# Attention and channel mix on one core: copies that two engines may do, and a merged sum on VectorE

## The chip, the cores and the metric

The kernel runs on one core of a Trainium2 chip. The metric is the device time of one execution in microseconds (us). The engines are TensorE (PE in the rows; its weight loads are PEld), VectorE (DVE), ScalarE (ACT), GpSimd (POOL) and SyncE (SP, which issues the DMAs).

## The reference

Eight batches of eight heads, 576 positions, 64 columns a head; then a channel mix with 512 model columns and 1024 hidden ones.

```python
scores = (q @ k.T) / sqrt(D)
cum = cumsum(maximum(s, 0))
bias = -(cum[:, :, :, None] - cum[:, :, None, :])
scores = where(causal, -1e6, scores + minimum(bias, 0))
attn = exp(scores - max); attn = attn / (sum(attn) + 1e-9)
x = (attn @ v), heads side by side            # 8 x 576 x 512
x_prev = x shifted by one position
xk = mu_k * x + (1 - mu_k) * x_prev           # xr the same with mu_r
v = maximum(xk @ w_k, 0) ** 2 @ w_v
out = sigmoid(xr @ w_r) * v
```

## The kernel before, in words

The program is first written as a list of tasks and then ordered. `Plan.add` (L113) records for each instruction its engine, its planned time in ns, what emits it, and which earlier tasks it depends on. `Plan.forward` (L135) goes through planned time: whichever engine is free first takes, of its tasks that are ready, the one due first. `Plan.backward` (L248) works out new due times from that order. `Plan.run` (L295) does this 30 times, keeps the order that ends earliest in planned time, and emits it. So each engine has a fixed queue in the order of the plan, and an instruction whose input is late holds up all behind it on its engine. A task has one engine: `act`, `dve`, `pool`, `pe` and `dma` (L363 to L385) record a task for ScalarE, VectorE, GpSimd, TensorE and SyncE with its planned duration. Until the first split scores are due, the plan fills idle time of TensorE with small matmuls on an identity (`one_idle`, L397).

Attention goes by visits, two heads each: the first batch in two halves (8 visits), the second batch (4 visits), the other six (24 visits). In the first 12 visits weights of the softmax are turned on TensorE and copied to SBUF by ScalarE (`turn_plain`, L1304: L1341, L1364). In the last 24 visits, most of the span, `split_scores` (L1086) is used. For each head it has four chains. Three are the query tiles 1 to 3 (`tile_`, L1159): the product of queries and keys into a bank of PSUM named s or t (two of each), the row minimum with the mask on VectorE (`least`, L1105), the exponent and its row sum on ScalarE (`exponents`, L1120), the reciprocal of the sum (`inverses`, L1129: a shifted copy on ScalarE, then a reciprocal on VectorE), and the weights as two f16 halves (`halves`, L1142): the first on ScalarE (L1147), the rest of it on VectorE (L1153), which reads the bank last and so frees it. The fourth chain (`last_and_first`, L1169) has the last tile and the 64 first queries packed into the same 128 rows, so on rows 64 to 127 two sums, of columns LAST and c, belong to one query. They are added across by two ScalarE instructions (L1202) with `upper_rows`, a column of zeros and ones, as scale; on rows 0 to 63 they stay apart. Then a DMA turns the halves (`turn_by_dma`, L1218) and TensorE sums the values (`sum_values`, L1242), whose result ScalarE scales into xT (L1297).

Before its turn, a visit is prepared by `split_qk` (L914) and `split_v` (L858): keys and queries are rounded into KH, KL and G by copies (L936 and L957 on ScalarE for the first two batches, L941 and L962 on GpSimd for the others; L951 on GpSimd), and GpSimd subtracts for the rests (L945, L966). Values are split on GpSimd (L867, L873, L875). The weights of the mix are unpacked ahead in `join` and `parts_of` (L701 on ScalarE, L708 on GpSimd).

The channel mix (`channel_mix`, L1522) goes in 18 chunks of 256 positions, and the plan fills them in between the attention's work as soon as a chunk's heads are done. Per chunk: the mix of x with its predecessor in a bank xp (L1568 on ScalarE, L1575 on VectorE), the f16 halves xh and xl (L1597 on ScalarE, L1601 on VectorE), the hidden product in a bank m (L1631), its relu r (L1643, ScalarE), square (L1653, VectorE), and halves kh (L1659, ScalarE) and kl (L1661, VectorE), the gate (L1675, L1687) and the output product (L1702, L1713). `MARGIN` (L1770) is part of a chunk's first due time.

Of the kernel before, what the change touches and what calls it, by code (L numbers as in the profile page):

```python
# [54 lines left out]
class Plan:  # L55
# [24 lines left out]
    def __init__(self):  # L80
        self.tasks, self.slots, self.due = [], {}, 0.0
        self.columns, self.idle, self.busy_from = {}, None, None
        self.quarters = {}
        self.issues = {}

# [48 lines left out]

    def forward(self, due):  # L135
# [15 lines left out]
        ready = {e: [] for e in engines}  # L151
        for i, t in enumerate(self.tasks):
            if not missing[i]:
                heapq.heappush(coming[t[0]], (0.0, i))
# [16 lines left out]
        while len(order) < n:  # L171
            best = None
            for e in engines:
                if ready[e]:
# [19 lines left out]
            while coming[e] and coming[e][0][0] <= s:  # L194
                _, i = heapq.heappop(coming[e])
                heapq.heappush(ready[e], (due[i], i))
            _, i = heapq.heappop(ready[e])
            if e == "PE" and ready[e]:
# [11 lines left out]
            _, ns, _, _, _, land = self.tasks[i]  # L210
            if e == "PE":
# [27 lines left out]
            for u in users[i]:  # L239
# [4 lines left out]
                if not missing[u]:  # L244
                    heapq.heappush(coming[self.tasks[u][0]], (ready_at[u], u))
        return order, start, max(done), emits

    def backward(self, start):  # L248
# [11 lines left out]
        for i in range(n):  # L260
            if not left[i]:
                heapq.heappush(coming[self.tasks[i][0]], (0.0, i))
        for _ in range(n):
# [15 lines left out]
            _, ns, _, deps, _, _ = self.tasks[i]  # L279
            free[e] = at[i] = s + (max(ns, self.issues.get(i, self.ISSUE)) if e == "SP" else ns)  # L280
            for d in deps:
                k, _, _, _, _, land = self.tasks[d]
# [10 lines left out]
    PASSES = 30  # L293

    def run(self):  # L295
        best = None
        due = [t[4] for t in self.tasks]
        for _ in range(self.PASSES):
# [3 lines left out]
            due = self.backward(found[1])  # L302
        order, _, _, emits = best
        for n, i in enumerate(order):
            for emit in emits.get(n, ()):
                emit()
            self.tasks[i][2]()
# [3 lines left out]
def forgetting_attention_then_channel_mix(  # L311
# [71 lines left out]

    def dma(emit, reads, writes, ns):
# [50 lines left out]
    upper_rows = fixed(const.tile([P, 1], F32, name="upper_rows"))  # L435
    for i in range(2):
        pool(
            lambda i=i: nc.gpsimd.memset(upper_rows.ap[64 * i : 64 * i + 64], 1.0 * i),
            [], [(upper_rows, i)], 1, 100,
        )  # L440
# [258 lines left out]
    def parts_of(block, whole):  # L699
        hi, lo = (block, 0), (block, 1)  # L700
        act(lambda: nc.scalar.copy(block.get()[:, 0], whole.get()), [whole], [hi], 512, 94)  # L701

        def first():
# [7 lines left out]
            [whole, hi], [lo], 512, 190, 2.21,  # L711
# [146 lines left out]
    def split_v(vn, V, scales):  # L858
# [3 lines left out]
        def whole():  # L862
# [10 lines left out]
        pool(lambda: nc.gpsimd.tensor_copy(part(0), whole()), [vn], [(V, 0)], n, 150)  # L873
        pool(
            lambda: nc.gpsimd.tensor_tensor(out=part(1), in0=whole(), in1=part(0), op=ALU.subtract),  # L875
            [vn, (V, 0)], [(V, 1)], n, 210, 2.21,
# [37 lines left out]
    def split_qk(b, hp, qs, k):  # L914
# [6 lines left out]
        for j in range(2):  # L921
# [11 lines left out]
            )  # L933
            if b < BY_DMA:
                act(
                    lambda own=own, K=K: nc.scalar.copy(K.get()[own], k.get()[own]),  # L936
                    [(k, j)], [(K, j)], nk, 90, quarters=(2 * j, 2 * j),
                )
            else:
                pool(  # L940
                    lambda own=own, K=K: nc.gpsimd.tensor_copy(K.get()[own], k.get()[own]),  # L941
                    [(k, j)], [(K, j)], nk, 150, 0.8333, (2 * j, 2 * j),
                )
# [4 lines left out]
                [(k, j), (K, j)], [(K, 1 - j)], nk, 210, 2.21, (2 * j, 2 - 2 * j),  # L948
            )
            pool(  # L950
                lambda own=own, KB=KB: nc.gpsimd.tensor_copy(KB.get()[0:64, 0:nk], k.get()[own]),  # L951
                [(k, j)], [(KB, 0)], nk, 150, 0.8333, (2 * j, 0),
            )
            x = qs[j]
            if b < BY_DMA:
                act(
                    lambda x=x, QQ=QQ: nc.scalar.copy(QQ.get(), x.get()),  # L957
                    [(x, 0), (x, 1)], [(QQ, 0), (QQ, 1)], nq, 90,
                )
            else:  # L960
                pool(
                    lambda x=x, QQ=QQ: nc.gpsimd.tensor_copy(QQ.get(), x.get()),  # L962
                    [(x, 0), (x, 1)], [(QQ, 0), (QQ, 1)], nq, 150,
                )
# [5 lines left out]
                [(x, 0), (QQ, 0)], [(QL, 0)], nq, 210, 2.21,  # L970
# [115 lines left out]
    def split_scores(passes, F, am, top):  # L1086
# [42 lines left out]
        def inverses(i, e, o):  # L1129
            act(  # L1130
                lambda: nc.scalar.activation(
                    rinv.get()[:, i:e], sums.get()[:, o : o + e - i], AF.Copy,
                    bias=1.0e-9 / HALF, scale=1.0 / HALF,
                ),
                [(sums, o + y - i) for y in range(i, e)], [(rinv, y) for y in range(i, e)], 1, 92,
            )
            dve(
                lambda: nc.vector.reciprocal(rinv.get()[:, i:e], rinv.get()[:, i:e]),  # L1138
                [], [(rinv, y) for y in range(i, e)], 1,
            )  # L1140

        def halves(ps, n, i, t, a, step):  # L1142
            def part(y):
                return F.get()[:, a + y * step : a + y * step + n]

            act(
                lambda: nc.scalar.activation(  # L1147
                    part(0), ps.get()[:, :n], AF.Copy, scale=rinv.get()[:, i : i + 1]
                ),
                [ps, (rinv, i)], [(F, (t, 0))], n, 144,  # L1150
# [9 lines left out]
        def tile_(t):  # L1160
# [5 lines left out]
            inverses(t, t + 1, t)  # L1166
            halves(ps, n, t, t, P * OB[t], P * (t + 1))

        def last_and_first():  # L1169
# [30 lines left out]
            for x, y in ((LAST, c), (c, LAST)):  # L1200
                act(
                    lambda x=x, y=y: nc.scalar.activation(  # L1202
                        sums.get()[:, x + 2 : x + 3], sums.get()[:, y : y + 1], AF.Identity,
                        scale=upper_rows.ap, bias=sums.get()[:, x : x + 1],
                    ),
                    [(sums, LAST), (sums, c), (upper_rows, 0), (upper_rows, 1)], [(sums, x + 2)], 1, 92,
# [759 lines left out]
```

## Time and profile before

| | us |
|---|---|
| median of 3 runs | 805.56 (805.26 to 806.03) |
| the profiled execution | 807.22 |
| its span, first to last instruction | 805.5 |
| mean granted TensorE clock in it | 0.991 |

| engine | busy us | share of the span | instructions |
|---|---|---|---|
| TensorE matmul | 768.5 | 95% | 5376 |
| TensorE weight load | 571.6 | 71% | 5376 |
| VectorE | 644.9 | 80% | 2031 |
| ScalarE | 638.0 | 79% | 1939 |
| GpSimd | 420.2 | 52% | 516 |

The time of an execution is a little longer than the span. The weight loader and the matmuls are two rows of one engine, and matmuls overlap in its pipe, so a busy TensorE can still have room. A mean over the span mixes stages: the weights' unpacking and the first heads up to about 160 us, attention with the mix in between up to about 700 us, and the rest of the mix alone.

### The profile page before, as it was taken

Reading aid. Unit: us, or ns where it says so; the run is one execution under the profiler, and the core shown is the slowest. Engines: PE = TensorE matmul, PEld = TensorE weight load, DVE = VectorE, ACT = ScalarE, POOL = GpSimd, SP = SyncE. Lnnn points to the kernel's source line nnn. Section 1 sums busy time; section 2 is a strip of 40 time slices with the busy share of each in tenths; the row PEclk is TensorE's granted clock in tenths of the full one; section 3 lists DMA queues with packets and bytes.
Section 4 is the critical chain, followed back from the end, with each engine's and each line's share of the span. In section 5 each row is a group of like instructions: output and inputs, shape, how many; then the busy total and the mean of one; then the engine's idle time right before and its main releaser. Section 6 shows DMA issues by size and latency. Waiting matters only on the chain. (4 is left out here: it accounts for less than half of the span.)

```text
span 805.5 us, 17398 instructions
## 1 busy us (share of the span) xinstructions
PE 768.5 (95%) x5376; PEld 571.6 (71%) x5376; DVE 644.9 (80%) x2031; ACT 638.0 (79%) x1939; POOL 420.2 (52%) x516
## 2 busy tenths in 40 slices
PE   9989899899989999999999999999999999999998
PEld 7766477676657676767676867676867686777785
DVE  7989976868988898888898988878987988646541
ACT  6799899778988798878888897979888988646521
POOL 6779685466576664564666655665555661000000
PEclk9999799999999999999999999999999999999999
DMA  7784444356896977996888979696879675511100
GB/s 252 214 263 135 157 126 132 114 124 148 180 194 169 183 178 181 202 172 163 164 184 159 218 162 200 164 216 156 208 157 198 158 138 84 133 48 40 40 27 26
DMA packets 220157, 124.16 MB, mean 154 GB/s; under 512 B 180192, under 2 KB 193504, under 8 KB 220064
## 3 DMA queue, kind: packets, MB, share of 16 engines
q1 hardware_dynamic: 220064, 123.06, 66.1%
q8 instruction: 42, 0.69, 0.4%
q14 instruction: 51, 0.42, 0.2%
HBM read 61.21 MB, written 19.33 MB: 100 GB/s over the span
## 5 line engine op out<-in xcount | busy, mean ns | idle before, releaser
L1631 PEld LDWEIGHTS <-w_k 128*128 128x128 f16 x1728 | 162.1, 98 | 35.1 <-issue 14.4
L1702 PE MATMUL m<-w_v,kh 128*128 128x512 f32 x528 | 179.2, 404 | 0.2 <-ACT g L1687 0.2
L1631 PE MATMUL m<-xh,w_k 128*128 128x256 f16 x976 | 175.5, 273 | 3.3 <-DVE kl L1661 2.7
L1631 PE MATMUL m<-xl,w_k 128*128 128x256 f16 x488 | 133.1, 273 | 0.1
L1702 PEld LDWEIGHTS m<-w_v,kh 128*128 128x128 f32 x528 | 98.3, 189 | 20.4 <-ACT g L1687 0.9
L1702 PE MATMUL m<-w_v,kl 128*128 128x512 f32 x264 | 106.7, 404 | 0.0
L945 POOL TENSOR_TENSOR KH<-raw,KH 64x576 fp32r<-64x576 f32 x64 | 90.4, 1413 | 10.1 <-ACT KH L936 5.7
L1568 ACT ACTIVATE xp<-x,shares 128x256 f32<-128x256 f32 (+3 forms) x184 | 78.4, 426 | 21.0 <-DVE xl L1601 11.4
L966 POOL TENSOR_TENSOR QL<-raw,G 64x576 fp32r<-64x576 f32 (+1 forms) x64 | 84.7, 1324 | 15.1 <-PE t L1095 7.7
L1575 DVE SCALAR_TENSOR_TENSOR xp<-x,shares,xp 128x256 f32<-128x256 f32 (+3 forms) x184 | 76.5, 416 | 17.8 <-ACT xp L1568 14.8
L1675 PE MATMUL m<-w_r,xh 128*128 128x512 f16 x264 | 84.5, 380 | 3.5 <-DVE kl L1661 3.0
L1153 DVE SCALAR_TENSOR_TENSOR W<-s,rinv,W 128x64 f16<-128x64 f32 (+2 forms) x144 | 64.9, 456 | 9.9 <-ACT W L1147 8.0
L1122 ACT ACTIVATE s<-s,nm 128x64 f32<-128x64 f32 (+2 forms) x144 | 61.8, 429 | 11.9 <-DVE nm L1107 10.3
L962 POOL CAST G<-raw 128x576 fp32r<-128x576 f32 x48 | 31.9, 665 | 73.6 <-issue 47.0
L1147 ACT ACTIVATE W<-s,rinv 128x64 f16<-128x64 f32 (+2 forms) x144 | 65.2, 460 | 6.3 <-DVE rinv L1138 5.3
L1153 DVE SCALAR_TENSOR_TENSOR W<-t,rinv,W 128x512 f16<-128x512 f32 (+1 forms) x96 | 61.6, 646 | 6.1 <-ACT W L1147 5.9
L1095 PE MATMUL s<-KH,G 128*128 128x64 f32 (+2 forms) x192 | 57.2, 312 | 8.3 <-DVE W L1153 6.4
L1122 ACT ACTIVATE t<-t,nm 128x512 f32<-128x512 f32 (+1 forms) x96 | 55.5, 578 | 6.3 <-DVE nm L1186 2.1
L1601 DVE TENSOR_TENSOR xl<-xp,xh 128x512 f16<-128x512 f32 x72 | 49.3, 685 | 12.6 <-ACT xh L1597 12.5
L1147 ACT ACTIVATE W<-t,rinv 128x512 f16<-128x512 f32 (+1 forms) x96 | 58.2, 614 | 0.9 <-DVE rinv L1138 0.7
L1107 DVE CUSTOM_DVE_ANT_0 t<-t,lower 128x512 f32<-128x512 f32 (+1 forms) x96 | 56.6, 596 | 2.8 <-PE t L1095 1.5
L1597 ACT CAST xh<-xp 128x512 f16<-128x512 f32 x72 | 42.4, 589 | 20.4 <-DVE xp L1575 20.3
(210 smaller groups left out, 1967.0 us busy)
## 6 DMA issues: line engine op xcount, KB each, us to landing
raw<-in_q SPq DMA_DIRECT2D x112, 144.0 KB
raw<-in_k SPq DMA_DIRECT2D x32, 288.0 KB
vn<-in_v SPq DMA_DIRECT2D x24, 384.0 KB
out<-g SPq DMA_DIRECT2D x36, 256.0 KB
x_d<-xT SPq DMA_DIRECT2D x28, 288.5 KB
x<-x_d SPq DMA_DIRECT2D x11, 514.0 KB
w_k<-in_moe_w_k SPq DMA_DIRECT2D x8, 512.0 KB
w_v<-in_moe_w_v SPq DMA_DIRECT2D x8, 512.0 KB
```

The lines of the kernel that those rows point to most:

```text
L945: lambda own=own, other=other, K=K: nc.gpsimd.tensor_tensor(out=K.get()[other], in0=k.get()[own], in1=f32(K.get()[own]), op=ALU.subtract),
L966: lambda x=x, QQ=QQ, QL=QL: nc.gpsimd.tensor_tensor(out=QL.get()[0:64, 0:nq], in0=x.get()[0:64], in1=f32(QQ.get()[0:64]), op=ALU.subtract,),
L1095: lambda x=x, G=G, K=K, r=r: nc.tensor.matmul(ps.get()[:m, :n], G.get()[:r, q : q + m], K.get()[:r, k0 : k0 + n], start=x == 0, stop=x == 1,),
L1107: lambda: nc.vector.tensor_tensor_reduce(out=ps.get()[:, :n], in0=ps.get()[:, :n], in1=mask(), scale=-SCALE, scalar=3.0e38, op0=ALU.add, o ...
L1122: lambda: nc.scalar.activation(ps.get()[:, :n], ps.get()[:, :n], AF.Exp, bias=nm.get()[:, i + o : i + o + 1], scale=-1.0, accum_out=sums.g ...
L1147: lambda: nc.scalar.activation(part(0), ps.get()[:, :n], AF.Copy, scale=rinv.get()[:, i : i + 1]),
L1153: lambda: nc.vector.scalar_tensor_tensor(out=part(1), in0=ps.get()[:, :n], scalar=rinv.get()[:, i : i + 1], in1=part(0), op0=ALU.mult, op1 ...
L1568: lambda z=z: nc.scalar.activation(to(*z), source(1, *z), AF.Copy, scale=share(0, c + z[0])),
L1575: lambda z=z: nc.vector.scalar_tensor_tensor(out=to(*z), in0=source(0, *z), scalar=share(1, c + z[0]), in1=to(*z), op0=ALU.mult, op1=ALU.a ...
L1631: lambda u=u, f=f, c=c, n=n, w=w, x=x: nc.tensor.matmul(ps.get()[:, u * CT : (u + 1) * CT], weight["k", c, f // 4].get()[:, w, f % 4 * P : ...
L1675: lambda c=c, n=n, x=x, w=w: nc.tensor.matmul(ps.get(), x.get()[:, c, ts], weight["r", c, 0].get()[:, w], start=c == 0 and n == 0, stop=c ...
L1702: lambda f=f, n=n, x=x, w=w: nc.tensor.matmul(ps.get(), x.get()[:, f, ts], weight["v", f, 0].get()[:, w], start=f == 0 and n == 0, stop=f ...
```

## The change

A task may get a second engine (`or_on`), with its own planned time and instruction. In `forward` such a task is offered to both engines, and the second takes it only if the first is not free within `LATER`, 300 ns. `backward` takes the engine chosen. The tasks that get a second engine: ScalarE's first halves, xT, turned blocks and corners, the first term of the mix, xh, relu and kh (or VectorE); the weights' first part and the early key and query copies (ScalarE, or GpSimd); the later key and query copies, KL and the values' first part (GpSimd, or ScalarE).

In `last_and_first`, one VectorE reduction adds the two sums on rows 64 to 127 into both columns of a second pair; ScalarE makes the shifted copy for rows 0 to 63 from the first pair and for the others from the second; one reciprocal follows for both columns. `upper_rows` goes. Some planned durations are altered, and `MARGIN` is 5000 instead of 10000.

```diff
+    def or_on(self, i, engine, ns, emit):
+        self.others[i] = engine, ns, emit
...
+        def offer(at, i):
+            heapq.heappush(coming[self.tasks[i][0]], (at, i))
+            if i in self.others:
+                heapq.heappush(coming[self.others[i][0]], (at, i))
...
             _, i = heapq.heappop(ready[e])
+            own = self.tasks[i][0]
+            if e != own and free[own] < s + self.LATER:
+                heapq.heappush(coming[e], (max(s, free[own]) + self.LATER, i))
+                continue
...
+            on[i] = e
+            if e != own:
+                ns = self.others[i][1]
...
     PASSES = 30
+    LATER = 300.0
...
+    def or_act(i, emit, n, extra=51):
+        plan.or_on(i, "ACT", n * 0.8333 + extra, emit)
+
+    def or_dve(i, emit, n, extra=70):
+        plan.or_on(i, "DVE", n / 0.96 + extra, emit)
+
+    def or_pool(i, emit, n, extra=150):
+        plan.or_on(i, "POOL", n * 0.8333 + extra, emit)
...
-        pool(lambda: nc.gpsimd.tensor_copy(part(0), whole()), [vn], [(V, 0)], n, 150)
+        or_act(
+            pool(lambda: nc.gpsimd.tensor_copy(part(0), whole()), [vn], [(V, 0)], n, 150),
+            lambda: nc.scalar.copy(part(0), whole()), n, 70,
+        )
...
-            act(
-                lambda: nc.scalar.activation(
-                    part(0), ps.get()[:, :n], AF.Copy, scale=rinv.get()[:, i : i + 1]
-                ),
-                [ps, (rinv, i)], [(F, (t, 0))], n, 144,
-            )
+            or_dve(
+                act(
+                    lambda: nc.scalar.activation(
+                        part(0), ps.get()[:, :n], AF.Copy, scale=rinv.get()[:, i : i + 1]
+                    ),
+                    [ps, (rinv, i)], [(F, (t, 0))], n, 144,
+                ),
+                lambda: nc.vector.tensor_scalar(
+                    out=part(0), in0=ps.get()[:, :n], scalar1=rinv.get()[:, i : i + 1],
+                    scalar2=None, op0=ALU.mult,
+                ),
+                n, 130,
+            )
...
-            for x, y in ((LAST, c), (c, LAST)):
+            dve(
+                lambda: nc.vector.tensor_reduce(
+                    out=upper(sums, LAST + 2, c + 3),
+                    in_=upper(sums, LAST, c + 1).unsqueeze(1).broadcast_to([64, 2, 2]),
+                    axis=mybir.AxisListType.X, op=ALU.add,
+                ),
+                [(sums, LAST), (sums, c)], [(sums, "u")], 4, quarters=(2, 2),
+            )
+            for rows, o, keys in (
+                (slice(0, 64), LAST, [LAST, c]), (slice(64, P), LAST + 2, ["u"]),
+            ):
                 act(
-                    lambda x=x, y=y: nc.scalar.activation(
-                        sums.get()[:, x + 2 : x + 3], sums.get()[:, y : y + 1], AF.Identity,
-                        scale=upper_rows.ap, bias=sums.get()[:, x : x + 1],
+                    lambda rows=rows, o=o: nc.scalar.activation(
+                        rinv.get()[rows, LAST : c + 1], sums.get()[rows, o : o + 2], AF.Copy,
+                        bias=1.0e-9 / HALF, scale=1.0 / HALF,
                     ),
...
-            inverses(LAST, c + 1, LAST + 2)
+            dve(
+                lambda: nc.vector.reciprocal(rinv.get()[:, LAST : c + 1], rinv.get()[:, LAST : c + 1]),
+                [(rinv, (LAST, "s")), (rinv, (LAST + 2, "s"))], [(rinv, LAST), (rinv, c)], 1,
+            )
...
-    MARGIN = 10000.0
+    MARGIN = 5000.0
```

The other pairs are of the same form. Lines of the changed kernel that the rows below name: L1165 exponents, L1174 and L1262 shifted copies (L1262 the merged chain's), L1191 and L1196 the first half on ScalarE and on VectorE, L1203 the second half, L1181 and L1269 reciprocals, L1251 the reduction, L1361 xT; of the preparation L973 and L1000 copies to KH and G on GpSimd, L988 to KL, L982 and L1009 the subtractions.

What stands in ScalarE's queue around the merged chain of one head, in the middle of attention; before:

```order
L1122 ACTIVATE t_232,sums_147<-t_232,nm_173 128x512
L1122 ACTIVATE s_145,sums_147<-s_145,nm_173 128x64
L1147 ACTIVATE W_2308<-s_152,rinv_2363 128x448
L1202 ACTIVATE sums_147<-sums_147,upper_rows 128x1 x2
L1643 ACTIVATE r_101<-m_272 128x512
L1131 ACTIVATE rinv_2167<-sums_147 128x2
```

and of the change, in such a head:

```order
L1165 ACTIVATE t_229,sums_174<-t_229,nm_233 128x512
L1165 ACTIVATE s_136,sums_174<-s_136,nm_233 128x64
L1262 ACTIVATE rinv_2361<-sums_174 64x2 x2
L1361 ACTIVATE xT_297<-s_142,scales_2419 128x64
L1361 ACTIVATE xT_297<-po_89,scales_2419 128x512
L1191 ACTIVATE W_2326<-s_136,rinv_2361 128x64
```

The pair that adds is gone; two copies on 64 rows each stand right behind the exponents, the second of which reads what VectorE adds. In 30 of the 48 heads the two stand side by side as here, in 18 something is between them.

VectorE's queue in attention, before:

```order
L1661 TENSOR_TENSOR kl_969<-m_272,kh_957 128x512
L1138 RECIPROCAL rinv_2167<-rinv_2167 128x1
L1107 ISA s_145,nm_173<-s_145,lower 128x448
L1107 ISA nm_173 128x1
L1653 SCALAR_TENSOR_TENSOR m_215<-m_215,scaled_1388,r_101 128x512
L1138 RECIPROCAL rinv_2167<-rinv_2167 128x1
L1153 SCALAR_TENSOR_TENSOR W_2136<-t_213,rinv_2167,W_2136 128x320
```

and of the change, where a first half is among the moved:

```order
L1269 RECIPROCAL rinv_2156<-rinv_2156 128x2
L1181 RECIPROCAL rinv_2156<-rinv_2156 128x1
L1659 SCALAR_TENSOR_TENSOR xp_332<-x_180,shares_780,xp_332 128x64
L1809 SCALAR_TENSOR_TENSOR g_430<-g_430,m_201 128x512
L1203 SCALAR_TENSOR_TENSOR W_2119<-s_142,rinv_2156,W_2119 128x64
L1196 TENSOR_SCALAR W_2119<-t_209,rinv_2156 128x320
L1688 TENSOR_TENSOR xl_837<-xp_332,xh_828 128x512
L1203 SCALAR_TENSOR_TENSOR W_2119<-t_229,rinv_2156,W_2119 128x512
L1203 SCALAR_TENSOR_TENSOR W_2119<-t_209,rinv_2156,W_2119 128x320
```

Here VectorE makes both halves of the 320 columns (L1196, then L1203); in all 24 of 240 first halves are VectorE's.

GpSimd's queue while a visit is prepared, before:

```order
L962 CAST G_577<-raw_514 128x576
L941 CAST KH_608<-raw_536 64x576
L966 TENSOR_TENSOR QL_226<-raw_514,G_577 64x576
L945 TENSOR_TENSOR KH_608<-raw_536,KH_608 64x576
L951 CAST KL_626<-raw_536 64x576
L962 CAST G_582<-raw_133 128x576
L941 CAST KH_622<-raw_514 64x576
```

and of the change:

```order
L982 TENSOR_TENSOR KH_769<-raw_480,KH_769 64x576
L988 CAST KL_633<-raw_480 64x576
L910 TENSOR_TENSOR V_2163<-vn_1016,V_2163 128x768
L1000 CAST G_640<-raw_498 128x576
L988 CAST KL_578<-raw_525 64x576
L1009 TENSOR_TENSOR QL_227<-raw_498,G_640 64x576
L982 TENSOR_TENSOR KH_600<-raw_525,KH_600 64x576
```

The copy to KH_600 no longer stands ahead of its subtraction: it is in ScalarE's queue.

## Rows read from the trace of the kernel before

**Rows 1.** The page: busy us (share of the span) and instructions of each engine.
```profile
PE 768.5 (95%) x5376; PEld 571.6 (71%) x5376; DVE 644.9 (80%) x2031; ACT 638.0 (79%) x1939; POOL 420.2 (52%) x516
```

**Rows 2.** Stretches: us, busy us (instructions) of each engine, PEclk, DMA share, GB/s.
```profile
20.00:40.00 20.00, 18.90 (x170) 15.53 (x170) 19.60 (x58) 14.97 (x53) 15.77 (x19) 1.00 0.70 214
...
40.00:80.00 40.00, 36.36 (x288) 27.14 (x284) 36.43 (x122) 37.38 (x103) 33.29 (x39) 0.96 0.64 198
80.00:120.00 40.00, 35.91 (x226) 24.91 (x227) 34.65 (x109) 37.72 (x107) 30.95 (x34) 0.87 0.46 147
...
160.00:680.00 520.00, 499.43 (x3482) 366.93 (x3482) 448.60 (x1470) 444.16 (x1408) 305.77 (x356) 1.00 0.81 173
...
560.00:600.00 40.00, 38.53 (x276) 29.06 (x275) 36.69 (x126) 35.98 (x116) 24.27 (x28) 1.00 0.85 189
...
720.00:805.50 85.50, 81.72 (x510) 62.77 (x508) 38.67 (x65) 33.18 (x63) 0.00 (x0) 1.00 0.10 35
```

**Rows 3.** The chain that ended last: start us, us, what (pieces of it).
```profile
521.43 0.69 ACT sums L1202 x2
...
702.66 2.13 PE po L1270 x28
...
704.86 5.29 PE m L1675 x24
...
801.84 0.69 DVE g L1713
```

**Rows 4.** Waits of PE and PEld, 160 to 704 us: us, times, longest us.
```profile
PE s L1095 <- DVE W L1153: 6.4, 17, 0.8
...
PE t L1095 <- DVE W L1153: 2.9, 6, 0.9
...
PEld s L1095 <- DVE W L1153: 18.3, 38, 1.1
...
PEld t L1095 <- DVE W L1153: 4.8, 11, 1.0
```

**Rows 5.** Waits of DVE, 160 to 704 us.
```profile
DVE rinv L1138 <- ACT rinv L1131: 22.6, 34, 2.4
DVE W L1153 <- ACT W L1147: 13.9, 35, 1.1
```

**Rows 6.** Groups by form, merged chain: out<-in xcount, busy us, mean ns, idle before.
```profile
L1202 ACT ACTIVATE sums<-sums,upper_rows 128x1 f32<-128x1 f32 x96 | 32.1, 388 | 0.1
...
L1131 ACT ACTIVATE rinv<-sums 128x2 f32<-128x2 f32 x48 | 10.0, 208 | 0.2
...
L1186 DVE TENSOR_REDUCE nm<-nm 64x2 f32<-64x4 f32 x48 | 7.4, 154 | 1.5
```

**Rows 7.** Groups by form: pairs of like work on ScalarE and VectorE.
```profile
L1601 DVE TENSOR_TENSOR xl<-xp,xh 128x512 f16<-128x512 f32 x72 | 49.3, 685 | 12.6 <-ACT xh L1597 12.5
...
L1568 ACT ACTIVATE xp<-x,shares 128x256 f32<-128x256 f32 x88 | 42.7, 485 | 13.3 <-DVE xl L1601 6.8 <-DMA x<-x_d 5.6
L1575 DVE SCALAR_TENSOR_TENSOR xp<-x,shares,xp 128x256 f32<-128x256 f32 x88 | 42.6, 484 | 12.4 <-ACT xp L1568 11.2
L1597 ACT CAST xh<-xp 128x512 f16<-128x512 f32 x72 | 42.4, 589 | 20.4 <-DVE xp L1575 20.3
...
L1153 DVE SCALAR_TENSOR_TENSOR W<-t,rinv,W 128x512 f16<-128x512 f32 x48 | 35.8, 746 | 2.3 <-ACT W L1147 2.2
...
L1147 ACT ACTIVATE W<-t,rinv 128x512 f16<-128x512 f32 x48 | 33.4, 695 | 0.0
```

**Rows 8.** Groups by form: the copy of a key on GpSimd and on ScalarE.
```profile
L941 POOL CAST KH<-raw 64x576 fp32r<-64x576 f32 x48 | 31.9, 664 | 23.3 <-PE s L1095 21.6 <-PE s L1022 0.5 <-DMA raw<-in_k 0.3
...
L936 ACT CAST KH<-raw 64x576 fp32r<-64x576 f32 x16 | 10.8, 673 | 0.5 <-PE s L1011 0.3
```

**Rows 9.** Timeline of PE, 90 to 92 us: start us, us, instruction [idle before].
```profile
90.25 0.40 PE L1022 MATMUL s<-KH,G 128*128 128x288 f32 x1 [0.36 <-DVE nm L1037]
...
91.99 0.61 PE L1022 MATMUL s<-KH,G 128*128 128x288 f32 x1 [0.29 <-DVE nm L1037]
```

More of the change, by code (lines that the diff above doesn't have):

```diff
@@ L173, in forward @@
             for e in engines:
+                while ready[e] and on[ready[e][0][1]]:
+                    heapq.heappop(ready[e])
+                while coming[e] and on[coming[e][0][1]]:
+                    heapq.heappop(coming[e])
                 if ready[e]:
@@ L700, in parts_of @@
         hi, lo = (block, 0), (block, 1)
-        act(lambda: nc.scalar.copy(block.get()[:, 0], whole.get()), [whole], [hi], 512, 94)
+        or_pool(
+            act(lambda: nc.scalar.copy(block.get()[:, 0], whole.get()), [whole], [hi], 512, 94),
+            lambda: nc.gpsimd.tensor_copy(block.get()[:, 0], whole.get()), 512,
+        )
         def first():
@@ L710, in parts_of @@
             ),
-            [whole, hi], [lo], 512, 190, 2.21,
+            [whole, hi], [lo], 512, 150, 2.0,
         )
@@ L1340, in block @@
             ks = range(kb, kb + n)
-            act(lambda: nc.scalar.copy(strips(ph), src()), [ps], [(ph, k) for k in ks], n * m)
+            or_dve(
+                act(lambda: nc.scalar.copy(strips(ph), src()), [ps], [(ph, k) for k in ks], n * m),
+                lambda: nc.vector.tensor_copy(strips(ph), src()), n * m,
+            )
         def strips_of(k0, n):
@@ L1362, in corner @@
                 n = max(n, 1)
-                act(
-                    lambda: nc.scalar.copy(strips_of(k, n), pairs_of(ps, at, lower, k and n)),
-                    [ps], [(ph, ("h", x)) for x in ks], 64 * n, quarters=(2 * lower, 0),
+                or_dve(
+                    act(
+                        lambda: nc.scalar.copy(strips_of(k, n), pairs_of(ps, at, lower, k and n)),
+                        [ps], [(ph, ("h", x)) for x in ks], 64 * n, quarters=(2 * lower, 0),
+                    ),
+                    lambda: nc.vector.tensor_copy(strips_of(k, n), pairs_of(ps, at, lower, k and n)),
+                    64 * n,
                 )
@@ L1583, in mixed @@
                     parts(*z[:2]) + [shares] + [(xm, ("a", *u)) for u in todo],
-                    [(xm, ("d", *z))], z[2], extra=250 if z is not todo[-1] else 130,
+                    [(xm, ("d", *z))], z[2], extra=130,
                 )
@@ L1594, in src @@
                 return xm.get().rearrange("p (c x) -> p c x", c=2)
-            act(
-                lambda: nc.scalar.copy(hi.get()[:, cc], src()),
-                parts, [(hi, c), (hi, c + 1)], 2 * CT,
+            or_dve(
+                act(
+                    lambda: nc.scalar.copy(hi.get()[:, cc], src()),
+                    parts, [(hi, c), (hi, c + 1)], 2 * CT,
+                ),
+                lambda: nc.vector.tensor_copy(hi.get()[:, cc], src()), 2 * CT,
             )
```

137 lines of the change are left out of this document (81 added, 56 removed).

## The prediction

> **What bounds the kernel now.** I read the busy times first, then the table of stretches, the chain that ended last, and the waits. TensorE is busy 95% of the span, VectorE 80%, ScalarE 79%, GpSimd 52% [rows 1]: TensorE is the bound, but not everywhere. In the table [rows 2] three stages are to be seen. From 720 us to the end PE is busy without a break until the last store, and the other engines are under half used. The chain [rows 3] shows why: the last attention sum is over at 704.9 us, and what follows, 97.0 us up to the last VectorE instruction, is three chunks of the channel mix back to back. The order of the changed kernel has the same work behind its last attention sum, 576 matmuls of the three products, as before. Nothing can be won there; what is won must be won before 704.9 us. From 160 to 680 us PE is busy 499.4 of 520 us, VectorE 448.6 (86%), ScalarE 444.2 (85%). From 40 to 120 us, with the weights being unpacked and the first heads done, ScalarE is the fullest, 37.4 and 37.7 of 40.
>
> In the middle stage PE waits mostly for one thing [rows 4]: a bank of scores (s or t) that becomes free when VectorE has written the second half of the weights (L1153). As idle time of PE that is 6.4 + 2.9 = 9.3 us; the weight loader, which runs ahead of the matmuls, waited 18.3 + 4.8 = 23.1 us. So late banks cost PE between 9.3 and 23.1 us; the upper figure is the nearer one, since a matmul in the pipe hides part of an idle array. VectorE in turn waits for ScalarE, at the reciprocals 22.6 us and at L1153 itself 13.9 us [rows 5]. It is a chain of two engines that hand work to and fro, each with idle time of its own.
>
> **The change part by part.**
>
> *The merge of the last tile's sums.* Before, ScalarE takes two instructions with two pointer operands (L1202, 0.388 us each) and one shifted copy of two columns (0.208), and VectorE one reciprocal [rows 6]. The chain has the pair as a piece of 0.69 us [rows 3]. After, VectorE does one reduction (0.154 by its twin L1186), ScalarE two shifted copies on 64 rows (taken at 0.208 each). Over 48 heads ScalarE gives up 32.1 us and takes one copy more per head, 48 x 0.208 = 10.0: 22 us off. VectorE takes 48 x 0.154 = 7.4 us on. The way from the exponent to the reciprocal loses 0.69 and gains 0.154, but there is one more handover from ScalarE to VectorE and back. This is a wait added: the upper copy waits for VectorE, and behind it in ScalarE's queue stand the copies of xT, the halves and other exponents. In 30 of the 48 heads the two copies stand side by side, so nothing of ScalarE's covers the reduction there.
>
> *ScalarE to VectorE.* The order shows 90 instructions moved: 59 inside the attention stage (23 first halves, 3 xT, 21 of the mix, 12 casts and squares' copies), 19 ahead of it (14 of them turned blocks) and 12 in the tail, where they cost nothing. By rows: a first half of 512 takes 0.695 on ScalarE; the nearest VectorE row is the second half of 512, 0.746, which has one input more and so is a ceiling. A cast of 512 takes 0.589 on ScalarE, 0.685 on VectorE (L1601, two inputs); a mix of 256 takes 0.485 and 0.484 [rows 7]. Form by form that comes to 30.9 us off ScalarE and at most 32.3 us on VectorE in the middle stage. [...]
>
> *GpSimd to ScalarE.* Inside the attention stage 49 copies move (19 KH, 12 KL, 17 G, one V). The casts of a key cost the same on both engines, 0.664 and 0.673 [rows 8], so ScalarE takes about 33 us on. GpSimd is not on PE's path (52% busy [rows 1]); its relief is worth nothing by itself.
>
> *The sum of loads, 160 to 680 us.* ScalarE: 444.2 - 22 - 30.9 + 33 = 424 us, 82% of the stretch. VectorE: 448.6 + 7.2 + 32.3 = 488 us; less some 5 us, since instructions in a row overlap by about 0.08 us (59 of them), 483: 93 to 94%. I go on with 486. So the change empties ScalarE a little and fills VectorE to where no 40 us slice of this stage stands now: the densest, 560 to 600 us, has 36.69 of 40, 91.7% [rows 2]. That is the number on which this prediction turns. Early on VectorE does get to 19.60 of 20 us, 98%, from 20 to 40 us [rows 2], so a queue with enough ready work can be that full.
>
> *What PE gets of it.* The planner gives an instruction to the second engine only where the first is not free within 0.3 us, so the moved ones fill idle time of VectorE, 71 us in this stage, of which 22.6 + 13.9 us were waits for ScalarE. PE loses at most 23.1 us to late banks. Nothing in the trace gives the share that goes; the ends are 0 and 23.1 us. I take a third, 8 us: the merge shortens one of a head's four chains, and of the first halves one in ten is moved. The fuller VectorE takes some back: I take 2 us, between 0 and the 9.6 us of the rival below. **Middle stage: -6 us.**
>
> *Ahead of it.* From 40 to 120 us some 13 us leave ScalarE (19 moved to VectorE, 13 copies to GpSimd against 5 from it), and VectorE, 71.1 us busy of the 80, takes at most 9 us on. The two together fall from 146.2 to about 142 us; were the work shared evenly at the 94% that ScalarE reaches, the 80 us would become 76. But VectorE has little room just there, so I take -2 us, between -4 and +3. [...] Five more of PE's filler matmuls stand in the new order, 88 for 83; they run where PE has nothing else and cost nothing.
>
> *Costs and margin.* The new planned durations and the margin of 5 instead of 10 us only set the order; what they do is in the rows compared. Nothing is added for them.
>
> **The sum.** -6 - 2 = -8 us on the profiled execution's 807.2 us (span 805.5 and 1.7 around it): 799.2. The median of the runs shown is 1.7 us lower, 805.56, so the forecast is 797.6, as a round figure **797.5 us**.
>
> **The rivals.** *VectorE becomes the bound (slower).* If in-order hand-overs do not let VectorE go beyond the 91.7% of the densest slice, 486 us of it need 486 / 0.917 = 530 us where there were 520: +9.6, and with the -2 ahead, 813 us. If it may be 93.5% full, the stage stays at 520; that is the point from which it decides. In its favour: the last link before a free bank is VectorE's, and the reduction of the merge is queued on it too. Against: 98% early on, and ScalarE, for which VectorE waited 36 us, becomes emptier. Chance 0.20, most of it between 807.2 and 813.
>
> *The waits only change places (no change).* ScalarE's queue and VectorE's are as intertwined as before, PE is handed its banks at the same pace, and the loads of x and of the turned weights, which the chain also holds, set the rest: 805.6 within 0.2%, 1.6 us, which is about what a measurement of this kernel can tell from no change. Chance 0.13.
>
> *All late banks go.* -23 and -4 ahead: 779 us. It needs VectorE 486 of 497 us busy, 98% over the whole stage. Chance 0.04 for anything under 789.
>
> **How the numbers follow.** The forecast, 789 to 803.9 us, has 0.63. Faster 0.63 + 0.04 = 0.67, same 0.13, slower 0.20. The low end, 789, is two thirds of the late banks and -2 ahead, 15.4 + 2 under 805.6 with a little to spare. For the high end I take in the no-change case and the first half of the slower rival, up to 809; above it about 0.1 is left, below 789 0.04.
>
> **What would show it.** Right: in the middle stage VectorE at 93 to 95% and ScalarE at about 82%, GpSimd near 52% of it; the loader's waits for L1153's successor (L1203) near 15 us for 23.1; VectorE's wait for ScalarE's reciprocal copies well under 22.6; the last attention sum some 8 us earlier and the tail after it again 97 us. The stage from 40 to 120 us should hold the same work in some 78 us. Wrong: the loader's waits for L1203 at 25 us or more, ScalarE idle in front of its second copy (L1262) because of the reduction (L1251), or ScalarE's waits for VectorE's minima grown; then VectorE is the bound and the time is over 805. [...]

## The result: slower, and where the time went

The changed kernel takes 816.19 us (median of 4 runs, 814.79 to 818.89), the kernel before 805.79 in the same session (805.26 to 807.82): ratio 1.0128, interval 1.0095 to 1.0161. The profiled execution took 816.99 us, with a span of 815.3. That is slower, and outside the predicted range.

The busy times of the changed kernel, against [rows 1]:
```profile
PE 765.3 (94%) x5375; PEld 569.0 (70%) x5375; DVE 692.9 (85%) x2184; ACT 616.5 (76%) x1829; POOL 392.4 (48%) x471
```
Work left ScalarE (21.5 us) and GpSimd (27.8), and VectorE got 48.0. The moves were made. The stretches (us, busy us of PE, PEld, DVE, ACT, POOL, then clock, DMA share, GB/s), against [rows 2]:
```profile
40.00:80.00 40.00, 34.77 (x282) 27.17 (x277) 38.48 (x121) 33.26 (x92) 36.35 (x43) 0.96 0.64 202
80.00:120.00 40.00, 37.38 (x264) 25.51 (x263) 38.17 (x123) 36.91 (x109) 33.45 (x38) 1.00 0.50 148
160.00:680.00 520.00, 489.57 (x3423) 358.19 (x3423) 472.96 (x1540) 430.20 (x1306) 267.84 (x296) 1.00 0.82 170
```
From 160 to 680 us PE has 489.6 us of work where it had 499.4: it lost 9.8 us there. VectorE went from 86 to 91%, not to the 93 or 94 foreseen. The last attention sum and the end, in the chain (start us, us, what), against [rows 3]:
```profile
712.51 2.13 PE po L1333 x28
714.71 5.07 PE m L1771 x23
...
811.61 0.69 DVE g L1809
```
The last sum starts at 712.51 us, 9.85 later than before, and from its successor to the last VectorE instruction it is 96.9 us for 97.0. So the whole loss lies ahead of 712 us. The waits there (160 to 705 us; us, times, longest), against [rows 4] and [rows 5]:
```profile
PE s L1138 <- DVE W L1203: 12.0, 16, 1.9
PE m L1718 <- DVE kl L1757: 6.4, 7, 2.4
...
PE m L1718 <- ACT xh L1682: 3.0, 2, 2.2
PE m L1771 <- DVE kl L1757: 2.4, 5, 0.7
PE m L1718 <- DVE xl L1688: 1.6, 2, 0.9
PE t L1138 <- DVE W L1203: 0.6, 3, 0.3
...
PEld s L1138 <- DVE W L1203: 27.6, 40, 2.2
...
PEld t L1138 <- DVE W L1203: 2.9, 7, 0.7
```
```profile
DVE W L1203 <- ACT W L1191: 7.6, 22, 0.9
DVE sums L1251 <- ACT s L1165: 7.1, 13, 1.4
...
DVE rinv L1181 <- ACT rinv L1174: 2.7, 4, 1.8
...
DVE rinv L1269 <- ACT rinv L1262: 1.7, 4, 0.5
```
VectorE waits less for ScalarE: for the reciprocals' copies 2.7 + 1.7 = 4.4 us instead of 22.6, with the reduction's wait for the exponents (7.1) 11.5; at L1203 7.6 instead of 13.9. Yet PE's banks come later: the loader's waits for them are 27.6 + 2.9 = 30.5 us, where they were 23.1. The engines are better fed and hand over later. The score banks are the smaller part of the loss. TensorE's own idle time for the hidden and gate products (bank m; the lines below are from the kernel before, 160 to 705 us) was 2.7 + 3.0 = 5.7 us and is 6.4 + 3.0 + 2.4 + 1.6 = 13.4; for the score banks it was 9.3 and is 12.6.
```profile
PE m L1675 <- DVE kl L1661: 3.0, 4, 1.1
...
PE m L1631 <- DVE kl L1661: 2.7, 8, 0.7
```
In e2 below, the other order, the two are 7.8 and 12.5 us, so which of them shows the loss depends on the order. ScalarE hardly waits for the merge's reduction (0.8 us), and its copies take 0.201 us where the prediction took 0.208. The two groups by form (out<-in xcount, busy us, mean ns, idle before):
```profile
L1262 ACT ACTIVATE rinv<-sums 64x2 f32<-64x2 f32 x96 | 19.3, 201 | 2.2 <-DVE sums L1251 0.8
...
L1251 DVE TENSOR_REDUCE sums<-sums 64x2 f32<-64x4 f32 x48 | 7.4, 153 | 8.3 <-ACT s L1165 7.1
```

**What the durations of single instructions hide.** Four mixes of one bank (L1659) in the timeline of VectorE, 370.0 to 371.8 us (start us, us, what; a line that folds several shows the shape of the first; the four have 192, 64, 192 and 64 columns):
```profile
370.01 1.53 DVE L1659 SCALAR_TENSOR_TENSOR xp<-x,shares,xp 128x192 f32<-128x192 f32 x4 [0.26 <-ACT xp L1646]
371.45 0.36 DVE L1150 CUSTOM_DVE_ANT_0 s<-s,lower 128x192 f32<-128x192 f32 x1
```
From the first start to the next instruction it is 1.44 us. The old planned durations, n/0.96 + 250 ns and + 130 for the last of a bank, come to 0.45 + 0.32 + 0.45 + 0.20 = 1.41 us. The new ones, + 130 for all, come to 1.05. Over the trace, a mix of 256 columns that has another instruction behind it on VectorE is followed after 398 ns in the median (256/0.96 + 130 = 397), but one that has a mix behind it after 522: the next mix starts some 35 ns after the end of the one ahead, where others start some 91 ns before it. In all 75 pairs the second mix waits for a semaphore that its own engine raises; they write the same bank. The new duration is right for a mix by itself and about 126 ns short (91 + 35) for each of the 75 mixes (of 192) that are followed by a mix: 75 x 0.126 = 9.5 us of VectorE that the planner doesn't know of. 56 of the 75 lie ahead of the end of the last attention sum: 7.1 us. The kernel before has 75 such pairs too, with the longer duration in the plan. On ScalarE's first terms of the mix (L1646) the same step is 511 ns, where the plan has 403.

### The profile page after: what moved, and what is told of

The parts are those of the page before. It is cut to its first block, busy times and chain, and to the rows that moved or that the text cites. A ratio compares the mean times of both kernels' runs of the same rounds, so it can differ in the third digit from the quotient of the medians.

```text
span 815.3 us, 17380 instructions
## 1 busy us (share of the span) xinstructions
PE 765.3 (94%) x5375; PEld 569.0 (70%) x5375; DVE 692.9 (85%) x2184; ACT 616.5 (76%) x1829; POOL 392.4 (48%) x471
## 4 chain that ended last, share of the span: by engine, by line
DVE 34%; PE 30%; ACT 15%; issue 9%; DMA 5%; POOL 4%; SPq 1%; ACTq 0%; DVEq 0%; POOLq 0%
PE m L1798 8%; DVE W L1203 6%; PE m L1718 4%; DVE xp L1659 4%; PE m L1771 4%; DVE t L1150 3%; ACT W L1191 3%; ACT s L1165 3%; ACT t L1165 3%; DVE s L1150 2%; DMA x<-x_d 2%; DVE m L1746 2%; PE t L1798 2%; ACT xp L1646 2%; DVE kl L1757 2%
## 5 line engine op out<-in xcount | busy, mean ns | idle before, releaser
L1718 PEld LDWEIGHTS <-w_k 128*128 128x128 f16 x1728 | 163.8, 99 | 46.9 <-issue 24.1
L1718 PE MATMUL m<-xh,w_k 128*128 128x256 f16 x976 | 179.6, 277 | 12.4 <-DVE kl L1757 8.7
L1718 PE MATMUL m<-xl,w_k 128*128 128x256 f16 x488 | 134.9, 277 | 1.6 <-DVE xl L1688 1.6
L982 POOL TENSOR_TENSOR KH<-raw,KH 64x576 fp32r<-64x576 f32 x64 | 90.3, 1411 | 4.9 <-ACT KH L970 0.5
L1009 POOL TENSOR_TENSOR QL<-raw,G 64x576 fp32r<-64x576 f32 (+1 forms) x64 | 84.9, 1326 | 3.9 <-ACT G L997 0.4
L1659 DVE SCALAR_TENSOR_TENSOR xp<-x,shares,xp 128x256 f32<-128x256 f32 (+3 forms) x184 | 76.5, 416 | 10.4 <-ACT xp L1646 7.2
L1646 ACT ACTIVATE xp<-x,shares 128x256 f32<-128x256 f32 (+3 forms) x145 | 61.2, 422 | 28.2 <-DVE xl L1688 11.2
L1165 ACT ACTIVATE s<-s,nm 128x64 f32<-128x64 f32 (+2 forms) x144 | 61.4, 426 | 12.2 <-DVE nm L1150 10.0
L1203 DVE SCALAR_TENSOR_TENSOR W<-s,rinv,W 128x64 f16<-128x64 f32 (+2 forms) x144 | 63.8, 454 | 4.1 <-ACT W L1191 3.6
L1203 DVE SCALAR_TENSOR_TENSOR W<-t,rinv,W 128x512 f16<-128x512 f32 (+1 forms) x96 | 61.7, 646 | 4.6 <-ACT W L1191 4.0
L1165 ACT ACTIVATE t<-t,nm 128x512 f32<-128x512 f32 (+1 forms) x96 | 55.4, 578 | 11.2 <-DVE nm L1236 5.9
L1191 ACT ACTIVATE W<-s,rinv 128x64 f16<-128x64 f32 (+2 forms) x125 | 56.8, 465 | 8.6 <-DVE rinv L1181 6.6
L973 POOL CAST KH<-raw 64x576 fp32r<-64x576 f32 x42 | 27.8, 661 | 73.4 <-PE s L1138 62.7
L1138 PEld LDWEIGHTS s<-KH,G 128*128 128x128 f32 (+1 forms) x192 | 33.6, 175 | 38.4 <-DVE W L1203 27.6
L1000 POOL CAST G<-raw 128x576 fp32r<-128x576 f32 (+1 forms) x40 | 26.3, 658 | 65.3 <-issue 40.8
L1798 PEld LDWEIGHTS m<-w_v,kl 128*128 128x128 f32 x264 | 49.7, 189 | 9.9
```

Source lines behind the costliest of these rows:

```text
L982: lambda own=own, other=other, K=K: nc.gpsimd.tensor_tensor(out=K.get()[other], in0=k.get()[own], in1=f32(K.get()[own]), op=ALU.subtract),
L1009: lambda x=x, QQ=QQ, QL=QL: nc.gpsimd.tensor_tensor(out=QL.get()[0:64, 0:nq], in0=x.get()[0:64], in1=f32(QQ.get()[0:64]), op=ALU.subtract,),
L1138: lambda x=x, G=G, K=K, r=r: nc.tensor.matmul(ps.get()[:m, :n], G.get()[:r, q : q + m], K.get()[:r, k0 : k0 + n], start=x == 0, stop=x == 1,),
L1165: lambda: nc.scalar.activation(ps.get()[:, :n], ps.get()[:, :n], AF.Exp, bias=nm.get()[:, i + o : i + o + 1], scale=-1.0, accum_out=sums.g ...
L1191: lambda: nc.scalar.activation(part(0), ps.get()[:, :n], AF.Copy, scale=rinv.get()[:, i : i + 1]),
L1203: lambda: nc.vector.scalar_tensor_tensor(out=part(1), in0=ps.get()[:, :n], scalar=rinv.get()[:, i : i + 1], in1=part(0), op0=ALU.mult, op1 ...
```

## The experiments

Theories: (A) the moves fill VectorE and ScalarE until banks come late, the slower rival; (B) the new planned durations are shorter than what the chip does, so other engines expect their banks too early; (C) the merge's handover, the margin, or one order's luck is the cause. One order's luck is possible because the planner takes its engines from a set, whose order isn't fixed, and it decides which of two free engines gets a step. The order rows ahead of the prediction are those of e2's order; the trace of the changed kernel has the counts of e1's (13 casts L1685 on VectorE, 12 in e2). All experiments have the list written out, in e1's order where nothing else is said. Before is 805.6 to 806.0 us in each session.

**e1 and e2, the two orders.**
```diff
-        engines = {t[0] for t in self.tasks}
+        engines = ['PE', 'ACT', 'DVE', 'POOL', 'SP']    # e1
+        engines = ['PE', 'POOL', 'ACT', 'DVE', 'SP']    # e2
```


> The changed kernel with the planner's list of engines written out (PE, ACT, DVE, POOL, SP) instead of a set, in the order that gives the instruction order that ran. Nothing else differs. Every theory expects 816 us (814 to 819); it is the base for the other runs. If it came out under 812, the 816 would not be a property of this order at all.

> The changed kernel with the list of engines written out as PE, POOL, ACT, DVE, SP: where two engines could begin a step at the same moment, another one gets it (24 first halves, 33 mix pairs and 12 cuts on VectorE instead of 29, 40 and 13). This is the order that the prediction showed. Theory A (VectorE and ScalarE are filled by the steps that were moved to them) and theory B (the new planned durations are too short for what the chip does, so the order can't be kept) both expect no large change, 812 to 818. Theory C (the loss is that one order's bad luck) expects 806 or less.

e1 took 815.08 us (ratio 1.0114, 1.0076 to 1.0152), e2 811.46 (1.0075, 1.0045 to 1.0105). The loss is there in both orders, 3.6 us apart. So a difference of under 5 us between two single kernels of this planner is not put down to an edit below.

**e3, no second engines, and e4, the old durations.**
```diff
     def or_on(self, i, engine, ns, emit):
-        self.others[i] = engine, ns, emit
+        return                                          # e3
...
-            [whole, hi], [lo], 512, 150, 2.0,
+            [whole, hi], [lo], 512, 190, 2.21,          # e4, the same for the other subtractions
-                        parts(*z[:2]) + [shares], [(xm, ("a", *z))], z[2], 190,
+                        parts(*z[:2]) + [shares], [(xm, ("a", *z))], z[2], 290,
-                    [(xm, ("d", *z))], z[2], extra=130,
+                    [(xm, ("d", *z))], z[2], extra=250 if z is not todo[-1] else 130,
-                [r, scaled], [ps], 2 * CT, extra=127,
+                [r, scaled], [ps], 2 * CT,
```


> The changed kernel with every step on its own engine (or_on returns at once); the merge, the new durations and the smaller margin stay. Theory A (the moves to VectorE and from GpSimd to ScalarE fill the engines that are waited for) expects the loss to go: 800 to 806. Theory B (durations too short) expects most of the loss to stay: 811 to 818, with GpSimd and VectorE behind their places in the order as before.

> The changed kernel with the planned durations of the kernel before (GpSimd's subtractions 2.21 n + 210, the mix 290 on ScalarE and 250 on VectorE, the read of the sums without its 127); the merge, the second engines and the smaller margin stay. Theory A expects the loss to stay, 812 to 818, since as many or more steps go to VectorE. Theory B expects it to go: 798 to 806, with the sum's waits for W of the first halves back under 25 us.

e3: 814.78 us (1.0116, 1.0097 to 1.0135), the whole loss, with VectorE no fuller than before (451.5 us from 160 to 680). Theory A falls. e4: 807.44 (1.0025, 1.0011 to 1.0039), 8 us better although 481.0 us of VectorE lie in that stretch, more than in e1. Theory B holds so far.

**e5, e6, e7: each part alone in the kernel before.** e5 has the new durations (e4's diff the other way round), e6 the diff of the merge, e7 that of the second engines.

> The kernel before with nothing but the new planned durations (engine list written out, which leaves its order as it was). Theory B (the loss comes from durations that are too short): 811 to 818, although not one instruction is added, removed or given to another engine. Rival C (durations only order the work and cost nothing by themselves, the loss is the merge's or the smaller margin's): 803 to 808.

> The kernel before with the merged sums alone (one VectorE addition of 64 rows, two 64-row copies on ScalarE, one reciprocal; durations, margin and engines as before). Theory B: 802 to 807, since the merge removes a VectorE and two ScalarE instructions a step. Rival C with the merge as the cause (a chain from VectorE to ScalarE and back, whose copies are planned too short): 811 to 817.

> The kernel before with the second engines alone (durations, margin and sums as before). Theory A, which run e3 has nearly taken away: 811 or more. Theory B: 798 to 807; if the moves are worth the 6 us that the prediction gave them, 799.

e5: 809.31 (1.0042, 1.0025 to 1.0059), slower, though under the 811 expected. e6: 802.53 (0.9965, 0.9949 to 0.9981), so the merge is not the cause. (The merge takes one ScalarE instruction a head off and puts one VectorE instruction on; the expectation has this wrong.) e7: 810.76 (1.0066, 1.004 to 1.0092): a miss for theory B, which had 807 or less. +3.7 - 3.1 + 5.2 = 5.8 us is not the 10 of the whole either; all three are near what an order's luck can do. Each alone settles little.

**e8, both mixes' durations alone.**
```diff
-                        parts(*z[:2]) + [shares], [(xm, ("a", *z))], z[2], 190,
+                        parts(*z[:2]) + [shares], [(xm, ("a", *z))], z[2], 290,
-                    [(xm, ("d", *z))], z[2], extra=130,
+                    [(xm, ("d", *z))], z[2], extra=250 if z is not todo[-1] else 130,
```


> The changed kernel with the mix's two durations alone as before (290 on ScalarE, 250 on VectorE but for the last); GpSimd's subtractions stay at the new, shorter ones. If the mix's durations are what the chip can't keep: 805 to 810. If GpSimd's are: 812 to 818, as in e1.

802.91 us (0.9964, 0.9939 to 0.9988): 12 us under e1, and under the kernel before. e10 repeats it with e2's list, e11 without second engines.

> e8 with the list of engines in the order of e2 (PE, POOL, ACT, DVE, SP), so that ties go another way. e1 and e2 are 815.1 and 811.5, which shows what ties alone do. If the mix's durations carry e8's gain: 799 to 807 here too, at least 4 us under e2. If e8 was one lucky order: 809 or more.

> e3 (no second engines) with the mix's two durations as before. Theory B: 798 to 805, ten or more under e3's 814.8; with the merge (e6: -3 us) and without the second engines (e7: +5 us) it may be the fastest of all. If the second engines are needed for e8's gain: 808 or more.

e10: 801.38 (0.9942, 0.9925 to 0.996), 10 under e2. e11: 805.43 (0.9996, 0.9977 to 1.0016), 9 under e3, a little above what was expected. In all three pairs the mix's durations carry it.

**e12 and e13, VectorE's mix alone and ScalarE's alone** (the second and the first edit of e8).

> e1 with VectorE's mix alone at 250 as before (ScalarE's stays at 190). If VectorE's wait is what the plan misses: 801 to 807. If it is ScalarE's (511 ns start to start where the plan has 403): 812 to 818. If each is half: 807 to 811.

> e1 with ScalarE's mix alone at 290 as before (VectorE's stays at 130). If VectorE's missing wait is the cause: 811 to 818, no better than e1 and e2. If ScalarE's counts as much (e12 was then a lucky order): 805 or less.

e12: 796.73 (0.9903, 0.9873 to 0.9933). e13: 812.6 (1.0083, 1.0068 to 1.0098). It is VectorE's duration; with ScalarE's alone the time is 2.5 us under e1, which is within an order's luck. Their stretch from 160 to 680 us, e12 and then e13:
```profile
160.00:680.00 520.00, 498.23 (x3475) 366.08 (x3473) 476.42 (x1562) 440.43 (x1341) 269.30 (x300) 1.00 0.84 173
```
```profile
160.00:680.00 520.00, 491.60 (x3407) 360.64 (x3406) 475.05 (x1537) 427.05 (x1298) 264.57 (x294) 0.99 0.82 171
```
VectorE is equally busy in both, 476 and 475 us, and PE differs by 6.6. How full VectorE is doesn't tell the good order from the bad one.

**e9, the wait in the plan.** The new durations stay; the planner is told that a mix follows the one ahead of it in its bank. Neither an instruction nor a wait is added on the chip. By the plan's own gaps a VectorE instruction that needs another of VectorE starts 131 ns after the time that the other is charged with (86 + 45), so 397 + 131 = 528 ns, near the 522 measured, and other work may be put between. The edit also holds for ScalarE's first terms, and by it 18 of these go to VectorE, where the changed kernel has 40; e12 and e15 (32 in both) change VectorE's duration alone.
```diff
+            def ahead(of, z):
+                n = todo.index(z)
+                return [(xm, (of, *todo[n - 1]))] if n else []
+
-                        parts(*z[:2]) + [shares], [(xm, ("a", *z))], z[2], 190,
+                        parts(*z[:2]) + [shares] + ahead("a", z), [(xm, ("a", *z))], z[2], 190,
-                    parts(*z[:2]) + [shares] + [(xm, ("a", *u)) for u in todo],
+                    parts(*z[:2]) + [shares] + [(xm, ("a", *u)) for u in todo] + ahead("d", z),
```


> The changed kernel, its new durations kept, in which the planner is only told that a mix of a bank follows the mix ahead of it in that bank (each reads the key that the one ahead writes). No instruction is added, and no wait that the chip doesn't already have: in the traces a VectorE mix that follows a mix starts 524 ns after it (256 columns), 397 if something else follows. If the loss comes from a wait that the plan has lost (theory B): 799 to 807, as near to e8's 802.9 as one order is to another. If e8 was only a luckier order, or the longer durations themselves helped: 811 to 818.

798.74 us (0.9906, 0.9881 to 0.9931), 16 under e1. VectorE in the timeline of e9, 181.1 to 183.2 us:
```profile
181.21 0.29 DVE L1663 SCALAR_TENSOR_TENSOR xp<-x,shares,xp 128x64 f32<-128x64 f32 x1
181.53 0.16 DVE L1562 TENSOR_REDUCE scaled<-tops 128x1 f32<-128x4 f32 x1
181.60 0.41 DVE L1663 SCALAR_TENSOR_TENSOR xp<-x,shares,xp 128x192 f32<-128x192 f32 x1
181.92 0.36 DVE L1150 CUSTOM_DVE_ANT_0 s<-s,lower 128x192 f32<-128x192 f32 x1
...
182.20 0.28 DVE L1663 SCALAR_TENSOR_TENSOR xp<-x,shares,xp 128x64 f32<-128x64 f32 x1
182.51 0.15 DVE L1251 TENSOR_REDUCE sums<-sums 64x2 f32<-64x4 f32 x1
182.70 0.42 DVE L1663 SCALAR_TENSOR_TENSOR xp<-x,shares,xp 128x192 f32<-128x192 f32 x1
```
Other work now stands in the hole behind a mix. 29 of the 192 mixes are still followed by a mix (32 in e14), for 75 in the changed kernel. The stretch and the loader's waits of e9:
```profile
160.00:680.00 520.00, 501.52 (x3488) 368.45 (x3487) 481.82 (x1586) 431.56 (x1330) 270.95 (x301) 1.00 0.82 173
```
```profile
PEld s L1138 <- DVE W L1203: 18.1, 38, 1.3
...
PEld t L1138 <- DVE W L1203: 1.4, 5, 0.5
```
PE is busy 501.5 us, 12 more than in the changed kernel and 2.1 more than before, with VectorE at 93%; the loader waits 19.5 us for banks, for 30.5.

e14 and e15 are e9 and e12 with e2's list.

> e9 (the wait between mixes in the plan, new durations kept) with the list of engines in the order of e2. Missing wait as the cause: 796 to 804, at least 7 us under e2's 811.5. e9 a lucky order: 807 or more.

> e12 (VectorE's mix at 250, ScalarE's at 190) with the list of engines in the order of e2. Missing wait as the cause: 795 to 804. e12 a lucky order: 807 or more.

e14: 797.78 (0.99, 0.9885 to 0.9915). e15: 801.4 (0.9945, 0.9924 to 0.9966). Neither is one order's luck. e14, e9 and e12 beat both kernels by about 1% of the time before.

**e16 to e18: what the wait needs beside it.** e16 is e5 with e9's edit, e17 is e3 with it, e18 is e9 with the last tile's sums as before.

> e5 (the kernel before with the new durations alone, 809.3) with the wait between the mixes in the plan; no merge, no second engines. Missing wait as the cause: 799 to 806, at least 3 us under e5. If the loss needs the second engines or the merge: 808 or more.

> The changed kernel with the wait between mixes in the plan and every step on its own engine. If the wait needs only the merge beside it: 797 to 804. If it needs the second engines: 807 to 815, as e16. Under e3's 814.8 in the first case by 10 or more.

> The changed kernel with the wait between mixes in the plan and the last tile's sums as before (two masked additions on ScalarE, one copy, one reciprocal). If the wait needs the merge beside it: 807 to 815. If it needs only the second engines: 797 to 804.

e16: 814.31 (1.0103, 1.0081 to 1.0125), a plain miss. e17: 809.85 (1.0038, 1.0015 to 1.0061), 5 under e3 where 10 were expected. e18: 802.74 (0.9953, 0.9935 to 0.997). So the wait in the plan needs the second engines more than the merge. With the merge and, but for the mix in the second row, the new durations (us):

| VectorE's mix in the plan | every step on its own engine | second engines |
|---|---|---|
| 126 ns short | e3 814.8 | e1 815.1, e2 811.5 |
| as before, ScalarE's mix too | e11 805.4 | e8 802.9, e10 801.4 |
| with its wait (e9's edit) | e17 809.9 | e9 798.7, e14 797.8 |

The second engines are worth nothing to 3 us in the first row, 3 to 4 in the second and 11 to 12 in the third. Without them the wait returns 5 us, within reach of an order's luck, and the old durations 9. Why e16 is slower than e5 stays open; in its trace VectorE waits for the copies of the unmerged sums again, longer than before [rows 5] (160 to 705 us):
```profile
DVE rinv L1138 <- ACT rinv L1131: 26.8, 36, 2.1
```
Not tried alone: the durations of GpSimd's subtractions, the 127 ns of the square (L1746), and the margin. The first two together are what e4 and e8 differ by, 807.4 and 802.9 us, so the new ones are no loss there.

## Why the prediction was wrong

**The step that failed** is the paragraph on costs and margin: "The new planned durations and the margin of 5 instead of 10 us only set the order; what they do is in the rows compared. Nothing is added for them." In this kernel the order is the time. One of those durations took 120 ns from a step whose back-to-back pace needs them. e12 puts that one number back: 816.2 (815.1 in e1) becomes 796.7, and e15 does so in the other order: 811.5 becomes 801.4. The prediction had the durations of a mix from [rows 7], 484 ns for 256 columns on VectorE, and never looked at what stands between the starts of two mixes. That VectorE's duration does it is shown (e9, e12, e14, e15 against e1, e2, e13). How the unplanned waits become the loss is not. 56 of them, 7.1 us, lie ahead of the last sum, which came 9.85 us later; but in e5 there are 61, 7.7 us, and in its trace that sum ends 1.4 us later than before (706.2 us). So the loss isn't the waits added up, and what a late mix holds up in a given order stays open.

**The order shown was one of several.** The rows that the prediction compared belong to e2, 811.5 us, not to the order that ran, e1, 815.1. That is 3.6 us of the miss at most; that ties depend on a set's order could be seen in the code.

**The rest of the sum was near, for the kernel that keeps the wait.** e9 and e14 come near what the prediction described:

| | forecast | e9 | e14 |
|---|---|---|---|
| time, us | 797.5 | 798.7 | 797.8 |
| VectorE busy to 680 us | 486 | 481.8 | 483.2 |
| ScalarE busy to 680 us | 424 | 431.6 | 436.7 |
| loader's waits for s and t of L1203 | near 15 | 19.5 | 15.6 |
| end of the last sum, 704.8 before | -8 | 698.2 | 696.5 |

So the sum of -8 us fits a plan that keeps the wait. That its parts do is not shown. 2.1 us of e9's gain and 1.6 of e14's came behind the last sum (98.6 and 99.1 us from there to the end, 100.7 before), where the prediction had nothing, and with the old durations the second engines alone cost 5.2 us (e7) where the merge alone gained 3.1 (e6). Part of the agreement is luck. One reading was too narrow: "PE waits mostly for one thing" holds for 9.3 of TensorE's 19.1 us of waits before; the products of the mix had 5.7, and in the kernel that ran these grew most.

**The rival with the right sign was right for another reason.** It gave 813 us because VectorE could not be over 91.7% full (486 / 0.917 is 530, so its +9.6 should be +10). e9 and e14 have it 93% full with PE at 501 to 502 us, and e3 loses the same 9 us with VectorE at 87%. Its chance of 0.20 was too low for "slower" as a whole, since the list had no case in which the plan itself becomes wrong. "The waits only change places" didn't happen, though e11's 805.4 looks like it. Of the signs named, the loader's waits over 25 us came true, and so did ScalarE's longer waits for the minima: 22.1 us before, 27.3 now (160 to 705 us; two lines of before, then four of the changed kernel; the other two of before are s 10.3 and nm 7.6).
```profile
ACT t L1122 <- DVE nm L1186: 2.1, 6, 0.7
ACT t L1122 <- DVE nm L1107: 2.1, 7, 0.5
```
```profile
ACT s L1165 <- DVE nm L1150: 10.0, 19, 1.4
...
ACT nm L1244 <- DVE nm L1150: 7.1, 12, 1.4
...
ACT t L1165 <- DVE nm L1236: 5.9, 11, 1.7
...
ACT t L1165 <- DVE nm L1150: 4.3, 8, 0.9
```
ScalarE's idle time before L1262 because of L1251 (0.8 us) did not.

**The stretch from 40 to 120 us.** No run shows the +3 us that the prediction had as the upper end for it. From 80 to 120 us the granted clock was 0.87 before and 1.00 in the changed kernel, e9 and e14, and PE had 37.4 us of work there in the changed kernel for 35.9.

**The moved steps' prices held.** VectorE's casts of 512 took 683 ns (685 taken from its subtraction), by form:
```profile
L1685 DVE CAST xh<-xp 128x512 f16<-128x512 f32 x13 | 8.9, 683 | 0.0
...
L1196 DVE TENSOR_SCALAR W<-t,rinv 128x512 f16<-128x512 f32 x3 | 2.2, 749 | 0.0
```
A first half of 512 took 749 ns, so the second half's 746, which the prediction took for a ceiling because of its further input, was simply the price.

## What to carry to other kernels

Where a planner or a hand-made schedule fixes the order on queues that run in order, a planned duration is an edit like any other: price it by the start-to-start times of the instruction in its neighbourhood (behind another of its kind, behind something else), not by its own length. If an engine's step waits for the one ahead of it, give the plan the wait and the short duration, so that other work can fill the hole (e9: 16 us under the short duration alone), or the longer duration, which did as much here (e12: 18 us). Neither is a cure by itself: without the merge and the second engines the wait gained nothing (e16). And pin whatever decides ties before comparing: two orders of the same plan were 3.6 us apart.

## What the chip showed that was not expected

A mix that waits for the mix ahead of it on VectorE starts about 125 ns later than other work does: behind a mix another instruction starts 91 ns before the mix ends in the median of 117 cases, a mix 35 ns after it, in all 75 pairs of the changed kernel. For ScalarE's first terms the step is about 95 ns: behind one the next instruction starts 63 ns before its end in the median, another first term 33 ns after it (medians of 103 and 49 cases).

In the trace of the changed kernel the merge's reduction on 64 rows (L1251) starts 30 to 32 ns after the instruction ahead of it ends in 33 of 48 cases, and the next starts 31 to 33 ns after its own end in 41, neither ever sooner; the reciprocal on 128 rows (L1269) overlaps both neighbours by 82 to 83 ns in the median. So the reduction takes about 217 ns of VectorE's queue (153 + 32 + 32), where the prediction charged 154. Why it leaves these gaps is not shown.
